# Attention scores of two heads on the two halves of TensorE's rows, and the bias added on VectorE

## The chip, the cores and the metric

The kernel runs on one core of a Trainium2 chip. The metric is the device time of one execution in microseconds (us); the median of the runs counts. A core has a matrix engine (TensorE, PE in the profile, with its weight loads listed apart as PEld), three engines that work element by element (VectorE = DVE, ScalarE = ACT, GpSimd = POOL), and the engine SP, which issues most DMA transfers here. Each engine carries out its own instructions in order; semaphores make one wait for another.

## What is computed

Three layers follow each other, all in float32 at the reference's side. The first is the one that is changed: attention with 4 batches, 8 heads, 576 positions, 64 numbers per head, a window of 128 positions and a bias that falls with distance.

```python
scores = scale * np.matmul(q, k.transpose(0, 1, 3, 2))
bias = slopes[:, None, None] * (-np.abs(rel).astype(np.float32))[None, :, :]
mask = (rel >= 0) & (rel < window)
scores = np.where(mask, scores + bias[None], -1000000000.0)
scores = scores - np.max(scores, axis=-1, keepdims=True)
attn = np.exp(scores)
attn = attn / (np.sum(attn, axis=-1, keepdims=True) + 1e-09)
return np.matmul(attn, v).astype(np.float32)
```

Its output (2304 tokens of 512 numbers) goes through a mixture of 8 experts, `out += P[:, e] * (relu(x @ w1[e]) @ w2[e])`, with weights P from an iterated normalisation over all tokens, and then through one more pair of matrices with a squared relu.

## The kernel before

**Stages.** The attention is worked pair by pair: 4 batches times 4 pairs of heads, in the order of `pairs`. While it runs, the first expert's products for the batches that are done are interleaved; after the last pair come the normalisation of P and the other experts. A run of one expert over one batch is 336 products, each one matmul of 288 columns in float16 with its own weight load (`products`, `hidden`, `layer`). They read `x`, `h` and `w`, write a PSUM bank `ps`, and ScalarE and VectorE add the banks up into `q` (`to_quarter`) and split the sums into two float16 halves for the next product.

**One pair of heads.** It has four units `u` of 128 queries. For each unit `score_ops` writes both heads' scores, 256 columns each, into one PSUM bank: first a matmul of the bias (bfloat16, `bia`) with the identity `identb`, then the scores on top. In the first two batches (`WHOLE = 2`) the scores are float32: `q` of both heads is stored with the other head's 64 rows set to zero, so each matmul uses all 128 rows of the array for one head. A float32 matmul shows as two records in the trace. In the last two batches `make_heads` first splits q and k into float16 halves on ScalarE and VectorE (or GpSimd), and each score is two float16 matmuls, with `qk`/`q` and `kl`.

**The softmax** (`unit`): VectorE takes the negated row maximum of both heads (`nm<-ps`, TENSOR_REDUCE), scales it, ScalarE computes the exponential out of PSUM into `e` and sums it into `sm` on the way (an ACTIVATE and an ACTIVATION_READ_ACCUMULATOR), VectorE adds a small number and inverts the sum, VectorE or ScalarE multiplies. In unit 0 this is done in two segments of 64 and 192 columns, in the others in one of 192. TensorE then transposes `e` into a bank, which is copied to `eT`, and when the pair's four units are there, two groups of 12 matmuls in all (`ps<-eT,v`) give the output (`values`, `take_x`).

**What sets the order.** A greedy scheduler (`Sched`) in the program issues, while the kernel is built, the operation with the lowest key of start time, lead and age, by costs that are written into the code (`START`, `RATE`, `PRICE`). Where an operation may go to two engines, it chooses by these costs. So every engine's order is fixed at build time.

**PSUM** has eight banks, shared out by `FRONT` until the first product run, then `MIDDLE` until the attention's end: P, Q, R for products, S for scores, T for transposes and part of the values, X for the rest of the values. In `MIDDLE` P, Q, R and X have one bank each, S and T two. Other rings: `e` five units (`RE`), `xq` one (`RX`).

## Time and profile before

| | us |
|---|---|
| runs: lowest, median, highest of 3 | 1879.82, 1884.69, 1884.86 |
| profiled execution, time | 1878.17 |
| profiled execution, span from first to last instruction | 1876.4 |
| TensorE busy | 1814.9 (97% of the span) |
| VectorE busy | 1576.8 (84%) |
| ScalarE busy | 1244.3 (66%) |
| GpSimd busy | 169.3 (9%) |

The time of the profiled execution is 1.8 us over its span and 6.5 us under the median. Busy time of TensorE counts an instruction from its start to its modelled end; matmuls are pipelined, so TensorE can be busy without being at its peak, and the distance from one start to the next says what an instruction costs in a dense stretch. The attention with the first products fills the first 285 us. The granted clock is 1.0 (2.4 GHz) there throughout.

### The profile page before, as it was taken

How to read it: one execution, taken by the hardware profiler on the slowest of the kernel's cores; microseconds unless marked ns; L12 is line 12 of the kernel's file. 1: busy time of each engine (PE TensorE's matmuls, PEld its weight loads, DVE VectorE, ACT ScalarE, POOL GpSimd, SP SyncE). 2: the span in 40 equal slices, each digit the busy share in tenths (PEclk: the TensorE clock that was granted, in tenths of full speed). 3: DMA queues.
4: the chain of work that ended last, by engine and by line, in shares of the span. 5: the costliest groups of instructions: out<-in, count | busy, mean ns of one | idle time of the engine just before them, and what ended most of it. 6: DMA issues, size and time to landing. Idle time of an engine off the chain costs nothing.

```text
span 1876.4 us, 38768 instructions
## 1 busy us (share of the span) xinstructions
PE 1814.9 (97%) x15077; PEld 1445.2 (77%) x15077; DVE 1576.8 (84%) x3475; ACT 1244.3 (66%) x3217; POOL 169.3 (9%) x207
## 2 busy tenths in 40 slices
PE   8899999898999999999999999999999999999999
PEld 7778777686777777777777777777777777777777
DVE  7987778897799999999999999999867777666666
ACT  7998876665566666666666667666646566666555
POOL 1110001100101212110012111111000000000000
PEclk9999999998999999999999999999999999999999
DMA  6554412438655535444453555345445585121321
GB/s 164 168 141 109 138 52 74 134 117 253 178 149 151 155 101 159 141 120 118 149 162 93 149 163 164 94 133 147 112 161 146 156 273 178 70 110 63 128 102 70
DMA packets 88233, 255.44 MB, mean 136 GB/s; under 512 B 26992, under 2 KB 35312, under 8 KB 88048
## 3 DMA queue, kind: packets, MB, share of 16 engines
q1 hardware_dynamic: 79984, 219.93, 35.2%
q0 software_dynamic: 8064, 33.03, 9.9%
q8 instruction: 118, 1.93, 0.4%
q14 instruction: 67, 0.55, 0.1%
HBM read 168.57 MB, written 84.35 MB: 135 GB/s over the span
## 4 chain that ended last, share of the span: by engine, by line
PE 60%; DVE 20%; DMA 8%; ACT 7%; issue 4%; SPq 0%; POOL 0%; DVEq 0%; ACTq 0%; POOLq 0%
PE ps L482 60%; DVE h L431 5%; DVE q L431 4%; DVE t L431 3%; ACT q L414 2%; DVE w L446 2%; DMA acc_s<-q 2%; DMA wst<-in_w 2%; DMA x_s<-wo 2%; ACT h L414 1%; ACT e L414 1%; DVE wz L431 1%; DVE wo L446 1%; ACT w L414 1%; DMA yw<-y_s 1%
## 5 line engine op out<-in xcount | busy, mean ns | idle before, releaser
L482 PEld LDWEIGHTS <-w 128*128 128x128 f16 x13440 | 1315.7, 98 | 395.9 <-issue 65.0
L482 PE MATMUL ps<-x,w 128*128 128x288 f16 x6720 | 861.2, 286 | 32.9 <-ACT q L414 19.1
L482 PE MATMUL ps<-h,w 128*128 128x288 f16 x6720 | 857.4, 286 | 14.4 <-DVE q L431 5.8
L414 ACT ACTIVATE q<-ps 128x288 f32<-128x288 f32 x926 | 364.5, 403 | 279.6 <-PE ps L482 268.6
L431 DVE TENSOR_TENSOR q<-ps,q 128x288 f32<-128x288 f32 x672 | 291.5, 449 | 106.5 <-PE ps L482 85.4
L414 ACT ACTIVATE q<-q 128x288 f32<-128x288 f32 x411 | 174.9, 440 | 95.2 <-DVE q L431 93.3
L414 ACT ACTIVATE h<-t 128x576 f16<-128x576 f32 x320 | 212.6, 679 | 30.8 <-DVE t L431 28.3
L414 ACT ACTIVATE h<-q 128x288 f16<-128x288 f32 x480 | 203.8, 439 | 4.4
L414 ACT ACTIVATE w<-wst 128x384 f16<-128x384 f32 (+1 forms) x256 | 141.1, 572 | 80.0 <-DMA wst<-in_w 38.0
L431 DVE TENSOR_TENSOR h<-q,h 128x288 f16<-128x288 f32 x384 | 173.3, 465 | 24.2 <-ACT h L414 23.3
L431 DVE TENSOR_TENSOR h<-t,h 128x576 f16<-128x576 f32 x256 | 188.5, 754 | 1.8 <-ACT h L414 0.9
L446 DVE SCALAR_TENSOR_TENSOR w<-wst,w 128x384 f16<-128x384 f32 (+1 forms) x256 | 161.4, 638 | 8.7 <-ACT w L414 8.4
L431 POOL TENSOR_TENSOR wst<-wst 128x256 f32<-128x256 f32 x107 | 97.1, 909 | 585.4 <-DVE wst L431 334.0
L431 DVE TENSOR_TENSOR t<-q,t 128x288 f32<-128x288 f32 x315 | 140.5, 456 | 1.9 <-ACT q L414 1.0
L431 DVE TENSOR_TENSOR t<-q 128x576 f32<-128x576 f32 x160 | 122.8, 770 | 6.2 <-ACT q L414 4.0
L431 DVE TENSOR_TENSOR q<-q,pb 128x576 f32<-128x576 f32 x108 | 83.6, 784 | 6.3 <-ACT q L414 5.6
L510 POOL DMA_DIRECT2D acc_s<-q x54 | 47.5, 907 | 431.2 <-DVE q L431 404.8
L414 ACT ACTIVATE e<-ps,nm 128x192 f32<-128x192 f32 (+1 forms) x160 | 64.1, 410 | 15.7 <-DVE nm L440 12.7
L431 DVE TENSOR_TENSOR wst<-wst 128x256 f32<-128x256 f32 x149 | 61.8, 426 | 2.4 <-POOL wst L431 0.5
L414 ACT ACTIVATE wo<-wz 128x384 f16<-128x384 f32 x64 | 36.8, 574 | 38.4 <-DVE wz L431 17.7
L453 DVE TENSOR_REDUCE nm<-ps 128x2 f32<-128x384 f32 (+1 forms) x80 | 38.3, 495 | 18.7 <-PE ps L482 18.4
L446 DVE SCALAR_TENSOR_TENSOR h<-q,h 128x288 f16<-128x288 f32 x96 | 43.1, 450 | 12.6 <-ACT h L414 12.6
(94 smaller groups left out, 1059.3 us busy)
## 6 DMA issues: line engine op xcount, KB each, us to landing
x<-x_s SPq DMA_DIRECT2D x56, 1008.0 KB, 4.8
wst<-in_w SPq DMA_DIRECT2D x64, 512.0 KB, 4.7
acc_s<-q POOLq DMA_DIRECT2D x54, 576.0 KB, 6.8
pb<-p_s SPq DMA_DIRECT2D x32, 288.0 KB, 5.5
yw<-in_win SPq DMA_DIRECT2D x16, 512.0 KB, 5.4
yw<-in_wout SPq DMA_DIRECT2D x16, 512.0 KB, 4.9
x_s<-x SPq DMA_DIRECT2D x8, 1008.0 KB, 4.9
win_s<-wo SPq DMA_DIRECT2D x16, 448.0 KB, 3.1
```

Of the source, the lines that this page charges most:

```text
L414: return Op("A", cost, reads, writes, lambda: nc.scalar.activation(out=out, in_=in_, func=func, scale=scale, **k))
L431: lambda: engine(e).tensor_tensor(out=out, in0=in0, in1=in1, op=op),
L446: lambda: nc.vector.scalar_tensor_tensor(out=out, in0=in0, scalar=s, in1=in1, op0=op0, op1=op1),
L453: lambda: nc.vector.tensor_reduce(out=out, in_=in_, axis=axis, op=op, **k),
L482: nc.tensor.matmul(o, l, r, start=start, stop=stop, skip_group_check=True)
L510: return Op("G", 1.04, [in_, out], [out], lambda: nc.gpsimd.dma_start(out=out, in_=in_, accum_op=ALU.add), m, ADDED)
```

## The change

- q and k of a pair are each loaded by one DMA into a tile of 128 rows: rows 0 to 63 are the first head, 64 to 127 the second. Nothing is padded or split; `make_heads` is gone, and so are `WHOLE`, the tiles `q0`, `q1`, `kl` and four memsets on GpSimd.
- A score matmul contracts 64 rows in float32, for all batches. The two heads alternate, head 0 on the array's rows 0 to 63, head 1 on rows 64 to 127, and write different banks. The bias matmuls are gone.
- Two units are worked together (`two`): two S banks, one per head, hold two units each. For each head and segment one VectorE instruction adds the bias to the scores out of PSUM, scales by -1/8, writes the result to `e` in SBUF and keeps its minimum for `nm` (`add_min`); the built program has a second VectorE instruction behind each that writes the minimum out. The scaling of `nm` is gone. ScalarE's exponential reads and writes `e` in SBUF.
- The small operations on `sm` take two units at once. `e` has three tiles of two units, `xq` two, `qk` six, `bia` three.
- PSUM: X is gone, both value groups take T. P has two banks in `MIDDLE` (0 and 7); S and T have four each in `FRONT` and two each in `MIDDLE`.

```diff
-FRONT = dict(zip("PQRSTX", (((0,), 1), ((1,), 1), ((2,), 1), ((0, 1, 3, 4), 4), ((2, 5, 6), 3), ((7,), 1))))
-MIDDLE = dict(zip("PQRSTX", (((0,), 1), ((1,), 1), ((2,), 1), ((3, 4), 2), ((5, 6), 2), ((7,), 1))))
+FRONT = dict(zip("PQRST", (((0,), 1), ((1,), 1), ((2,), 1), ((2, 5, 6, 7), 4), ((0, 1, 3, 4), 4))))
+MIDDLE = dict(zip("PQRST", (((0, 7), 2), ((1,), 1), ((2,), 1), ((5, 6), 2), ((3, 4), 2))))
...
-RE, RX = 5, 1
+RE, RX = 3, 2
...
+    def add_min(out, least, in0, in1, scale):
+
+        return Op(
+            "D", START["D"] + 0.06 + RATE["D"] * size(out), [in0, in1], [out, least],
+            lambda: nc.vector.tensor_tensor_reduce(
+                out=out, in0=in0, in1=in1, scale=scale, scalar=3.0e38, op0=ALU.add, op1=ALU.min, accum_out=least
+            ),
+        )
...
-                        for a in range(2):
-                            yield dma(Q[64 * a : 64 * a + 64, a], qT[b, 2 * p + a])
...
+                    for src in (qT, kT):
+                        x = yield Need(r_qk)
+                        yield dma(x, src[b, h].rearrange("h d s -> (h d) s"))
...
+            def score_ops(at, us, ps):
+
+                Q, K = qk[at]
+                seq = []
+                for j, u in enumerate(us):
+                    q, k = 128 * u + 64, 128 * u - 64
+                    if u == 0:
+                        parts = [(0, 128, 0, 64, 0, 0), (0, 128, 64, 192, q, 0)]
+                    else:
+                        parts = [(0, 64, 0, 64, q, k), (64, 64, 0, 64, q + 64, k + 192), (0, 128, 64, 128, q, k + 64)]
+                    for p0, n, c0, w_, q0, k0 in parts:
+                        for a in range(2):
+                            r = slice(64 * a, 64 * a + 64)
+                            c = 256 * j + c0
+                            seq.append((ps[a][p0 : p0 + n, c : c + w_], Q[r, q0 : q0 + n], K[r, k0 : k0 + w_], True, True))
+                return mms(seq, together=2)
...
-                for i, (c0, c1) in enumerate(segs):
-                    yield reduce(nm[:, 2 * i : 2 * i + 2], ps.rearrange("p (a c) -> p a c", a=2)[:, :, 64 * c0 : 64 * c1], AX.X, ALU.max, True)
-                yield ts(nm[:, :m], nm[:, :m], ISQ, ALU.mult)
...
-                for i, x in each:
-                    yield act(e[x], f[x], AF.Exp, ISQ, nm[:, i : i + 1], sm[:, i : i + 1])
...
+                for i in range(m + 1):
+                    if i < m:
+                        n, a, j, s = each[i]
+                        at_bias = slice(2, 3) if us[j] == 0 and s.start == 0 else s
+                        f = ps[a][:, 256 * j : 256 * j + 256].rearrange("p (c k) -> p c k", k=64)
+                        yield add_min(e[:, j, s, a], nm[:, n : n + 1], f[:, s], t[:, at_bias, a], -ISQ)
+                    if i:
+                        n, a, j, s = each[i - 1]
+                        yield act(e[:, j, s, a], e[:, j, s, a], AF.Exp, -1.0, nm[:, n : n + 1], sm[:, n : n + 1])
...
-                    for r_, part in zip((bank["X"], bank["T"]), parts):
-                        x = yield Need(r_)
+                    for part in parts:
+                        x = yield Need(bank["T"])
```

How the change moves instructions, at three places. First TensorE at the program's start, where `ps_165` and `ps_166` are the banks of units 0 and 1 before, and `ps_160` and `ps_161` those of heads 0 and 1 after. Before:

```order
L482 LDWEIGHTS identb_70
L482 MATMUL ps_165<-bia_163,identb_70 128x2x192
L482 MATMUL ps_165<-qk32_161,q0_144 128x64 x2
L482 MATMUL ps_165<-qk32_161,q0_144 128x192 x2
L482 LDWEIGHTS identb_70
L482 MATMUL ps_166<-bia_163,identb_70 128x2x192
L482 MATMUL ps_166<-qk32_161,q0_144 64x64 x4
L482 MATMUL ps_166<-qk32_161,q0_144 128x128 x2
```

After, the same place:

```order
L491 MATMUL ps_160<-qk_155,qk_151 128x64
L491 MATMUL ps_161<-qk_155,qk_151 128x64
L491 MATMUL ps_160<-qk_155,qk_151 128x192
L491 MATMUL ps_161<-qk_155,qk_151 128x192
L491 MATMUL ps_160<-qk_155,qk_151 64x64
L491 MATMUL ps_161<-qk_155,qk_151 64x64
```

The bias matmuls are gone, and the heads alternate between two banks. Second VectorE in the middle of the attention, among the first expert's products. Before:

```order
L453 TENSOR_REDUCE nm<-ps 128x2 x2
L440 TENSOR_SCALAR nm<-nm 128x2
L431 TENSOR_TENSOR t<-q,t 128x288
L431 TENSOR_TENSOR q_144<-qk_2161,q_144 64x1152
L440 TENSOR_SCALAR nm<-nm 128x4
L431 TENSOR_TENSOR h_2283<-q,h_2283 128x288
L431 TENSOR_TENSOR kl<-qk_2178,q_144 128x1152
```

After, at a similar place (ISA is `add_min`, and behind each the instruction that writes its minimum):

```order
L452 ISA e,nm<-ps,bia 128x3x64
L452 ISA nm 128x1
L465 RECIPROCAL sm<-sm 128x4
L430 TENSOR_TENSOR q<-ps,q 128x288
L430 TENSOR_TENSOR h_551<-q,h_551 128x288
L452 ISA e,nm<-ps,bia 128x3x64
L452 ISA nm 128x1
```

One reduction for two heads has become an add and a write-out per head, and the two splits of 1152 numbers (`q_144`, `kl`) are gone. Third SP's queue of DMA issues at the start. Before:

```order
L506 DMA wgf<-in_wg 128x4x8
L506 DMA q_144<-in_qT 64x576 x2
L506 DMA qk_161<-in_kT 128x576
L506 DMA bia<-in_bias 128x512
L506 DMA q_145<-in_qT 64x576 x2
```

After:

```order
L515 DMA wgf<-in_wg 128x4x8
L515 DMA qk<-in_qT 128x576
L515 DMA qk<-in_kT 128x576
L515 DMA bia<-in_bias 128x512
L515 DMA qk<-in_qT 128x576
```

The first pair's loads take one issue less, and three pairs are loaded ahead of `v` where two were.

## Rows read from the trace of the kernel before

**Rows 1.** By stretch: length, busy PE, PEld, DVE, ACT, POOL (instructions), clock, DMA share, GB/s.
```profile
0.00:58.00 58.00, 48.50 (x422) 41.67 (x423) 44.73 (x148) 46.87 (x170) 11.56 (x22) 1.00 0.64 172
58.00:112.00 54.00, 49.44 (x471) 41.20 (x470) 50.46 (x130) 49.17 (x155) 10.41 (x11) 1.00 0.51 135
112.00:250.00 138.00, 132.79 (x1368) 109.75 (x1365) 108.69 (x281) 120.00 (x376) 2.86 (x3) 1.00 0.46 130
...
600.00:700.00 100.00, 98.80 (x802) 78.18 (x801) 94.48 (x193) 61.73 (x153) 16.28 (x21) 1.00 0.47 131
```
**Rows 2.** Chain that ended last, by time: start, duration, engine and line; 58 to 250.
```profile
75.83 0.67 DVE h L431
...
97.85 1.33 ACT e L414 x7
...
121.77 5.62 PE ps L482 x51
```
**Rows 3.** What TensorE waited for, 58 to 285: us in total, times, longest.
```profile
PE ps L482 <- ACT q L414: 7.5, 12, 1.2
```
**Rows 4.** Instructions in order of time at the start: start, duration, engine.
```profile
3.14 0.43 SPq L506 DMA_DIRECT2D bia<-in_bias  x1
...
6.58 0.58 PE L482 MATMUL ps<-bia,identb 128*128 128x128 bf16 x2 [6.58 <-DMA bia<-in_bias]
...
10.39 0.31 ACT L414 ACTIVATE e<-ps,nm 128x64 f32<-128x64 f32 x1 [7.50 <-DVE nm L440]
```
**Rows 5.** TensorE in order of time, a float32 unit at 16.7 us.
```profile
16.73 0.33 PE L482 MATMUL ps<-bia,identb 128*128 128x384 bf16 x1
16.98 1.10 PE L482 MATMUL ps<-qk,q 128*64 128x64 f32 x12
17.92 0.49 PE L480 MATMUL ps<-ident,e 128*128 128x128 f32 x3
```
**Rows 6.** TensorE in order of time, a float16 unit at 230.1 us.
```profile
230.13 0.33 PE L482 MATMUL ps<-bia,identb 128*128 128x384 bf16 x1
...
230.51 0.21 PE L482 MATMUL ps<-kl,q 128*64 128x64 f16 x2
230.65 0.23 PE L482 MATMUL ps<-q 128*128 128x128 f16 x1
230.71 0.22 PE L482 MATMUL ps<-kl,q 128*128 128x128 f16 x1
...
230.88 0.33 PE L482 MATMUL ps<-bia,identb 128*128 128x384 bf16 x1
```
**Rows 7.** VectorE groups to 290 us: count, busy us, mean ns, idle time before them.
```profile
L453 DVE TENSOR_REDUCE nm<-ps 128x2 f32<-128x384 f32 x64 | 35.0, 547 | 7.7 <-PE ps L482 7.5
...
L453 DVE TENSOR_REDUCE nm<-ps 128x2 f32<-128x128 f32 x16 | 4.6, 286 | 11.0 <-PE ps L482 10.8
...
L440 DVE TENSOR_SCALAR nm<-nm 128x4 f32<-128x4 f32 (+1 forms) x64 | 11.3, 177 | 0.7
...
L440 DVE TENSOR_SCALAR sm<-sm 128x4 f32<-128x4 f32 (+1 forms) x64 | 10.7, 167 | 6.3 <-ACT e L414 6.0
L457 DVE RECIPROCAL sm<-sm 128x4 f32<-128x4 f32 (+1 forms) x64 | 10.4, 163 | 0.8
```
**Rows 8.** ScalarE groups to 290 us, same columns.
```profile
L414 ACT ACTIVATE e<-ps,nm 128x192 f32<-128x192 f32 (+1 forms) x160 | 64.1, 410 | 15.7 <-DVE nm L440 12.7 <-PE ps L482 2.4 <-DVE sm L440 0.4
L414 ACT ACTIVATE e<-e,sm 128x192 f32<-128x192 f32 (+1 forms) x122 | 48.8, 438 | 3.4 <-DVE sm L457 2.1 <-DVE sm L440 1.1
L414 ACT ACTIVATION_READ_ACCUMULATOR e<-ps,nm 128x1 f32 x160 | 34.8, 217 | 0.0
```
**Rows 9.** Instructions on `qk` alone by stretch: each engine's busy time (instructions).
```profile
0.00:58.00 58.00, 26.65 (x239) 21.65 (x240) 0.00 (x0) 0.00 (x0) 1.00 0.64 172
58.00:112.00 54.00, 11.67 (x116) 9.13 (x114) 2.70 (x2) 2.33 (x2) 1.00 0.51 135
112.00:250.00 138.00, 0.00 (x0) 0.00 (x0) 18.95 (x14) 16.26 (x14) 1.00 0.46 130
```

More of the change, by code (lines that the diff above doesn't have):

```diff
@@ L895, in unit @@
                 e = yield Need(r_e)
                 sm = yield Need(r_sm)
[L897 to L900 removed]
+                t = bias_in[at].rearrange("p (a c k) -> p c a k", a=2, k=64)
+                segs = [(j, s) for j, u in enumerate(us) for s in (((0, 1), (1, 4)) if u == 0 else ((0, 3),))]
@@ new lines, in two @@
+                each = [(2 * i + a, a, j, slice(*s)) for i, (j, s) in enumerate(segs) for a in range(2)]
+                m = len(each)
+                for i in range(m + 1):
[7 more added lines that the diff above has]
+                        yield act(e[:, j, s, a], e[:, j, s, a], AF.Exp, -1.0, nm[:, n : n + 1], sm[:, n : n + 1])
@@ L1067, in attn_moe_relu2 @@
             spawn(load_heads(), LEAD_ATT)
-            spawn(make_heads(), LEAD_ATT)
             spawn(units(), LEAD_ATT)
```

137 lines of the change are left out of this document (46 added, 91 removed).

## The prediction

> **What bounds the kernel now.** I read three views in this order. First the busy times by stretch [rows 1], where I call 0 to 58 us stretch A (batch 0 and part of batch 1, no products yet), 58 to 112 stretch B (the rest of batch 1, first products) and 112 to 250 stretch C (batches 2 and 3 in float16, products all along). See who is nearest to the whole length. In A it is ScalarE: its first exponential starts at 10.39 us [rows 4], and of the 47.6 us from there it is busy for some 45. In B VectorE (50.5 of 54) and ScalarE (49.2) are both nearly full, TensorE is at 49.4. In C TensorE is busy for 132.8 of 138, VectorE for 108.7, ScalarE for 120.0.
>
> Second the chain that ended last [rows 2]: up to about 112 us it alternates between short pieces of VectorE and ScalarE, and from 121 us on TensorE's pieces of several microseconds make it up. So time saved on TensorE is worth its full length in C, only as much as the other two engines allow in B, and nothing in A. Third TensorE's waits [rows 3]: from 58 to 285 us its products waited 7.5 us for ScalarE to empty a bank.
>
> After the attention little can move by the order itself: from product 2232 of 13440 on, TensorE's order is the same in both programs, and so are VectorE's last 2485 instructions. The attention's end has 900 products ahead of it before and 984 after. I therefore take the change in time from the first part alone and let it shift the rest.
>
> **The change part by part.** One float32 unit now: the bias matmul starts at 16.73, the scores at 16.98, the next work at 17.92 [rows 5]. That is 1.19 us a unit, 0.94 of it for scores. A pair has four units (unit 0 has other shapes, I take it as alike): 4.76 us, of which 3.76 are scores. A float16 unit goes from 230.13 to 230.88 [rows 6], 0.75, so 3.0 a pair. After the change every pair has 22 float32 matmuls of 64 rows, alternating between the halves. No row shows two matmuls on different halves, so the price lies between 3.76 (no overlap) and 1.88 (full). I take 1.88, since neighbours in the new order never share rows of the array or a bank. Then a float32 pair saves 2.88 and a float16 pair 1.12.
>
> Where the pairs lie follows from the float32 score records [rows 9]: 239 in A and 116 in B, at 44 a pair 5.4 pairs and 2.6. So TensorE is relieved of 15.6 us in A, 7.5 in B and 8 x 1.12 = 9.0 in C.
>
> *A change of shape costs.* In a float16 unit the step from the last 64-column matmuls to the first of 128 columns is 0.14 us from row to row, while 128-column ones follow each other in 0.06 [rows 6]: about 0.08 more. Before, a pair has six such changes; afterwards nine (four in units 0 and 1, five in 2 and 3). Three more, times 10.6 pairs in B and C, times 0.08, is 2.5 us lost.
>
> *VectorE.* Gone are the maxima (35.0 + 4.6), the scaling of `nm` (11.3) and half of the work on `sm` ((10.7 + 10.4) / 2), in all 61.5 us [rows 7]; and the splits, 21.65 us [rows 9]. Added are 128 adds of 192 columns and 32 of 64. The two reductions give (547 - 286) / 256 = 1.02 ns per column and so 0.35 and 0.22 us, 51.8 us. To it come 160 write-outs of the minimum: nothing at the least (hidden in the next instruction's start), at the most what ScalarE's write-out takes, 0.217 [rows 8]; I take 0.163, that of VectorE's own small operations [rows 7], 26.1 us. For adds as long as ScalarE's exponentials (0.410) with that write-out the sum is 160 x 0.627 = 100.3. So a pair costs VectorE (77.9 - 61.5) / 16 = 1.0 us more, with bounds of -0.6 and +2.4.
>
> *ScalarE.* The exponential reads SBUF instead of PSUM; the nearest pair of rows is 438 against 410 ns [rows 8], +0.28 us a pair. The splits go, 18.59 us, of which 2.33 in B and 16.26 in C [rows 9].
>
> *What this makes of A.* TensorE's 15.6 us are cover there, not path. Added are 5.4 x (1.03 + 0.28) = 7.1 us on the two engines that are nearly full. Half of it is 3.5 us of time; VectorE idles for 13.3 us in A [rows 1], but most of that lies before the first scores are done, a little over 9 us; the 4 us left, and some 2 on ScalarE, could take most of the 7.1 and leave 0.5. I take 2 us lost.
>
> *B.* TensorE's 7.5 us can only be used by products, and these need VectorE. From 600 to 700 us, 802 matmuls go with 94.48 us of VectorE [rows 1], 0.118 each. In B VectorE has 3.5 us left; the adds (2.6 x 1.03) and the split that goes (2.70) cancel. That is 30 products, and at 98.80 / 802 = 0.123 us each of TensorE they give 3.6 us later. The new order plans more (330 products, not 252, ahead of batch 1's last values); what VectorE can't follow only lengthens B.
>
> *C.* 9.0 us, all on the path: VectorE and ScalarE lose 18.95 and 16.26 us there and gain 8.2 and 2.2, so neither becomes the bound.
>
> *Start.* TensorE waited until 6.58 for the bias, whose issue ended at 3.57 [rows 4], 3.0 us before. Now it needs q and k alone, each in one issue, so two issues of about half a microsecond less stand ahead; by the same 3.0 us it starts near 5.5. The first exponential, 3.8 us behind, needed two bias matmuls, eight records, two reductions and a scaling, now one matmul pair and one add. I take 2 us, of 1 to 3. The first expert's weights have 14 issues ahead of them on SP, where there were 13, so they don't move; `v` is behind one more pair's loads, about 1.5 us later, and is not read before the first transposes are copied. GpSimd's four memsets hide under these loads.
>
> *Banks.* P has a second bank while products and attention mix. Of the 7.5 us [rows 3] I take 3, of 0 to 7.5. Against it stands that `two` holds both S banks, so no second set of scores can start, and that the values share T; a `two` with half a pair's scores (0.94) and five adds with write-outs (5 x 0.5) holds them for some 3.5 us plus waits, twice a pair, and eight pairs have 138 us, so products cover it.
>
> *The sum:* 9.0 + 3.6 + 2 + 3 - 2.5 - 2 = 13.1 us. The profiled execution took 1878.17, so it would take 1865.1. It lies 6.5 us under the median of the runs shown, 1884.69, and these spread over 5 us; on the median I forecast **1872**.
>
> The Trainium skill, "TensorE: Matmul & The Clock Gate", Part 3, says that matmuls in different row groups run at the same time, but reports 3.07 times for four row tiles, not four. No run here shows that. If two halves gave the same share, 1.53, a pair would cost 2.46, C would give 4.3 instead of 9.0, and the time would be an estimate of 1876.
>
> **The rivals.** *The halves take turns (slower).* If float32 matmuls on the two halves don't overlap, a pair costs 3.76: C gets 8 x 0.76 = 6.1 us longer, B gains 2.6, and with the other terms (+2.5, +2, -5) it is 3.0 us slower, 1888. If each of the 22 moves between halves then also costs 0.08 like a change of shape, a pair costs 5.5: C +20.2, B +2.0, in all +21.7, 1906. It decides from a pair price of 3.5 us on (no gain), and from 4.0 it is slower by 0.3%. For it: no row shows an overlap. Against it: rows and banks are separate. The Trainium skill, "TensorEngine Tiling (Array Packing)", Key Properties, says that changing the mode drains the engine, but not changing the tile within it. The gap at the change of shape agrees; by that rule the moves between halves cost nothing, and this rival ends at 1888, not at 1906.
>
> *The adds cost VectorE what they save (no change).* At 100.3 us they are 38.8 over what goes, 2.4 a pair. In A that is 13.1 us against some 4 of idle time, +9; B gives nothing back; C still gives 9.0 and start and banks 5, the shape changes take 2.5: 2.4 faster, 1882. For it: VectorE and ScalarE alternate on the chain in A and B, and all product sums queue behind the adds on VectorE. Against it: the reductions' own rows give an add 0.35 us, not 0.41.
>
> *All of TensorE's time is used (faster).* 15.6 + 7.5 + 9.0 + 2 + 3 - 2.5 = 34.6, 1850. For it: VectorE and ScalarE choose between themselves who normalises and copies. Against it: they are full in A.
>
> **How the numbers follow.** A measurement can tell about 0.3%, 5.7 us, from no change. Forecast 0.60, by its bounds from 1859 to 1879, so all but faster (0.58, and 0.02 within). All of TensorE's time 0.12, faster. Adds 0.15, within 0.3%. Taking turns 0.13, slower 0.09 and within 0.04. That is faster 0.70, same 0.21, slower 0.09. For 8 in 10 the range takes in the forecast, the adds and half of the most favourable case, 1852 to 1886, and leaves out the halves' turns.
>
> **What would show it.** In the new profile the two records of head 0 and head 1 start closer together than the 0.94 / 12 = 0.08 us of now, and a unit of scores takes under 0.6 us, if they overlap; 0.9 would speak for turns. A VectorE add of 192 columns of 0.35 us and a write-out that moves the next start by at most 0.16 bear out the price; 0.4 each would give the second rival. The attention's last transposes end about 13 us earlier for the products done by then, C's length shrinks most, A's hardly. The prediction is wrong if the granted clock falls in A, where TensorE now has gaps, or if what follows the attention waits for its loads and gives back what came before.

## The result and the profile after

The changed kernel takes 1894.46 us (1890.06 to 1895.96), 1.0063 times the kernel before, 95% interval 1.0049 to 1.0078: slower by some 12 us. The five runs of before beside it have a median of 1880.33, 4 us under the 1884.69 that the prediction started from. The prediction said 1872, range 1852 to 1886. Its profiled execution has a span of 1893.6 us against 1876.4.

By stretch, columns as in [rows 1]:

```profile
0.00:58.00 58.00, 44.38 (x339) 36.32 (x340) 38.93 (x167) 42.92 (x152) 8.81 (x17) 0.91 0.59 170
58.00:112.00 54.00, 49.14 (x445) 39.41 (x444) 46.73 (x139) 48.28 (x146) 8.80 (x10) 0.87 0.32 106
112.00:250.00 138.00, 136.03 (x1356) 111.64 (x1356) 92.53 (x339) 112.43 (x367) 0.00 (x0) 1.00 0.31 98
350.00:400.00 50.00, 40.99 (x313) 31.38 (x312) 48.42 (x129) 32.69 (x77) 1.46 (x2) 0.93 0.39 129
450.00:500.00 50.00, 38.61 (x264) 28.25 (x264) 30.56 (x57) 17.27 (x42) 1.95 (x3) 0.80 0.83 261
```

The same two last stretches in the kernel before:

```profile
350.00:400.00 50.00, 45.70 (x367) 35.56 (x366) 48.70 (x128) 36.38 (x89) 5.83 (x5) 1.00 0.35 119
450.00:500.00 50.00, 46.57 (x356) 35.70 (x355) 35.49 (x70) 23.83 (x61) 3.45 (x4) 0.95 0.88 254
```

The first three rows answer [rows 1]. VectorE and ScalarE are busy for less in all three, in A partly because less of the work is done by 58 us (the table below); TensorE is at least as full in C as before. The last two lie after the attention and hold the loss: TensorE is busy for 41.0 and 38.6 of 50 us, against 45.7 and 46.6.

VectorE's new instructions, from the groups (columns as in [rows 7]):

```profile
L452 DVE CUSTOM_DVE_ANT_0 e<-ps,bia 128x192 f32<-128x192 f32 x128 | 42.4, 351 | 5.5 <-PE ps L491 5.1 <-PE ps L489 0.4
L452 DVE DVE_READ_ACCUMULATOR2_ANT nm<- 128x1 f32 x160 | 13.4, 84 | 0.0
```

And the start, from the timeline (start, length, engine, line, operation, idle time before):

```profile
5.40 5.19 PE L491 MATMUL ps<-qk 64*128 64x64 f32 x46 [5.40 <-DMA qk<-in_kT]
8.28 0.35 ACT L413 ACTIVATE e<-e,nm 128x64 f32<-128x64 f32 x1 [5.29 <-DVE nm L452]
```

The first scores start at 5.40 and the first exponential at 8.28, against 6.58 and 10.39 [rows 4].

**Where the time goes.** I follow TensorE's lost time: the start of product n less n times 0.1229 us, its pace in after where nothing waits (814 products start between 1600 and 1700 us). It counts the attention's own matmuls and all waits. The end of the attention is the start of its last `ps<-eT,v` matmul.

| lost time, us | before | after |
|---|---|---|
| at the end of batch 0 | 54.8 | 58.5 |
| batch 1 | 47.6 | 49.5 |
| batches 2 and 3 | 65.5 | 58.2 |
| at the attention's end | 167.9 | 166.2 |
| from there to product 1500 | 9.3 | 4.6 |
| products 1500 to 1560 | 2.1 | 12.1 |
| products 2130 to 2250 | 11.2 | 18.9 |
| at product 2490 | 193.0 | 204.2 |

So the attention gained 1.7 us instead of 13.1, and two waits behind it lost 18 more than before. At product 2490 the kernel is 11.2 us late, about the difference of the runs; another 5 us go between products 10400 and 11200 in this one execution.

Not all of the two losses is standing still. Behind each wait the granted clock is 0.5 (1.2 GHz) for a while, 6.8 us from 367.3 and 17.1 us from 449.2, and there 18 and 44 products start up to twice as far apart; that is 2.0 of the 12.1 and 5.0 of the 18.9 us (before: 0.2 and 2.9). The rows of after, columns as in [rows 1]:

```profile
350.00:375.00 25.00, 15.99 (x107) 11.31 (x106) 24.96 (x63) 16.95 (x39) 0.00 (x0) 0.86 0.44 146
450.00:475.00 25.00, 15.84 (x94) 10.86 (x94) 16.70 (x33) 10.85 (x26) 0.00 (x0) 0.67 0.75 216
```

The attention ends with 984 products ahead of it where it had 900, and in clock time it ends later, at 287 against 278.5 us. What hangs on it, from the timelines of before and then of after:

```profile
275.54 3.19 PE L482 MATMUL ps<-eT,v 128*128 128x64 f32 x24
287.34 0.30 DVE L453 TENSOR_REDUCE m<-P 128x1 f32<-128x144 f32 x1
289.01 0.27 PE L480 MATMUL ps<-ident,m 128*1 128x128 f32 x1
293.45 0.41 ACT L414 ACTIVATE P<-P,m 128x144 f32<-128x144 f32 x1 [1.12 <-DVE m L440]
```

```profile
286.08 1.32 PE L491 MATMUL ps<-eT,v 128*128 128x64 f32 x10
297.06 1.90 PE L491 MATMUL ps<-wgs,x 128*128 128x16 f16 x60
300.72 0.29 DVE L461 TENSOR_REDUCE m<-P 128x1 f32<-128x144 f32 x1
311.41 0.27 PE L489 MATMUL ps<-ident,m 128*1 128x128 f32 x1
321.88 0.41 ACT L413 ACTIVATE P<-P,m 128x144 f32<-128x144 f32 x1
```

The maximum of P (`m<-P`) comes 13 us later, its transposition 22 us later, since 102 products stand between the last logits and it, where 24 did; the exponential that opens the gate's eight rounds comes 28 us later. Then TensorE's waits in after from 350 to 400 us, and from 440 to 500 us (what waited, for what: us, times, longest):

```profile
PE ps L491 <- DVE cs L461: 4.1, 1, 4.1
PE ps L491 <- DVE q L430: 3.9, 2, 3.6
```

```profile
PE ps L491 <- ACT q L413: 11.0, 2, 10.2
PE ps L491 <- DVE q L430: 1.2, 1, 1.2
PE ps L491 <- ACT h L413: 1.2, 1, 1.2
PE ps L491 <- DVE h L430: 1.0, 1, 1.0
```

The 4.1 us of the first list are a wait for the gate itself: its column sum `cs` on VectorE is late, and the matmul that sums it over the rows stands in TensorE's order among the products (start, length, idle time before):

```profile
368.76 0.60 PE L491 MATMUL ps<-cs,ones 128*128 128x8 f32 x2 [4.15 <-DVE cs L461]
```

The 3.6 us are a wait for VectorE's sum of an earlier product. No wait named here is for weights, and VectorE is busy for 73.4 of the 75 us from 300 on. The wait of 10.2 us is for a buffer `q`: ScalarE, which TensorE waits for, itself waits there for the transfer `acc_s<-q`, which by the code goes out only when that result has been weighted with the gate's result and the early result of its batch has been stored.

### The profile page after: what moved, and what is told of

It is laid out like the page before. It is cut to its first block, busy times and chain, and to the rows that moved or that the text cites. A ratio compares the mean times of both kernels' runs of the same rounds, so it can differ in the third digit from the quotient of the medians.

```text
span 1893.6 us, 38623 instructions
## 1 busy us (share of the span) xinstructions
PE 1820.4 (96%) x14997; PEld 1446.5 (76%) x14997; DVE 1550.4 (82%) x3579; ACT 1236.5 (65%) x3201; POOL 158.2 (8%) x195
## 4 chain that ended last, share of the span: by engine, by line
PE 68%; DVE 17%; DMA 7%; ACT 6%; issue 2%; SPq 0%; POOL 0%; DVEq 0%; ACTq 0%; POOLq 0%
PE ps L491 67%; DVE h L430 5%; DVE t L430 3%; DVE q L430 3%; ACT q L413 2%; DMA acc_s<-q 2%; ACT h L413 2%; DVE w L445 2%; DMA x_s<-wo 2%; DMA yw<-in_win 1%; PE ps L489 1%; ACT e L413 1%; DVE wo L445 1%; DVE wz L430 1%; DMA yw<-y_s 1%
## 5 line engine op out<-in xcount | busy, mean ns | idle before, releaser
L430 DVE TENSOR_TENSOR h<-q,h 128x288 f16<-128x288 f32 x384 | 171.9, 462 | 24.5 <-ACT h L413 23.8
L445 DVE SCALAR_TENSOR_TENSOR w<-wst,w 128x512 f16<-128x512 f32 (+1 forms) x256 | 160.8, 637 | 3.2 <-ACT w L413 2.9
L519 POOL DMA_DIRECT2D acc_s<-q x54 | 47.6, 906 | 444.8 <-DVE q L430 367.2
L413 ACT ACTIVATE e<-e,nm 128x192 f32<-128x192 f32 (+1 forms) x160 | 67.8, 425 | 10.9 <-DVE nm L452 10.6
L452 DVE CUSTOM_DVE_ANT_0 e<-ps,bia 128x192 f32<-128x192 f32 (+1 forms) x160 | 47.8, 325 | 22.8 <-PE ps L491 22.2
L491 PE MATMUL ps<-qk 64*64 64x64 f32 (+3 forms) x704 | 56.0, 311 | 8.0 <-DMA qk<-in_kT 5.4
L413 ACT ACTIVATE wo<-wz 128x384 f16<-128x384 f32 x64 | 36.8, 574 | 39.3 <-DVE wz L430 17.5
```

Of the source, the lines that this page charges most:

```text
L413: return Op("A", cost, reads, writes, lambda: nc.scalar.activation(out=out, in_=in_, func=func, scale=scale, **k))
L430: lambda: engine(e).tensor_tensor(out=out, in0=in0, in1=in1, op=op),
L445: lambda: nc.vector.scalar_tensor_tensor(out=out, in0=in0, scalar=s, in1=in1, op0=op0, op1=op1),
L452: lambda: nc.vector.tensor_tensor_reduce(out=out, in0=in0, in1=in1, scale=scale, scalar=3.0e38, op0=ALU.add, op1=ALU.min, accum_out=least),
L491: nc.tensor.matmul(o, l, r, start=start, stop=stop, skip_group_check=True)
L519: return Op("G", 1.04, [in_, out], [out], lambda: nc.gpsimd.dma_start(out=out, in_=in_, accum_op=ALU.add), m, ADDED)
```

## The experiments

**How two halves and shapes are priced.** Two kernels hold the same score matmuls as the changed one, in another order inside a set; all else stays.

```diff
+                wide = lambda x: x[1].shape[-1] == 128
+                seq.sort(key=lambda x: wide(x) if us[0] else not wide(x))
                 return mms(seq, together=2)
```

> The changed kernel with the same matmuls in another order within each set of scores: those of one shape stand together (in units 0 and 1 the 128-column stationary tiles first, in units 2 and 3 the 64-column ones first), still alternating between the heads, so that a pair has 4 changes of shape inside its scores instead of 9. Everything else stands where it stood. If a change of shape costs about 0.23 us (the gaps that TensorE's weight loads show there), a pair's scores take some 1.7 to 2.2 us instead of 2.84, and the time falls by 4 to 8 us if TensorE's time in the attention is what counts, 1886 to 1890, or by less than 2 us if the later wait for the gate sets the end. If a change costs 0.08 as the prediction had it, the pair takes 2.4 or more and the time stays within 2 us of the changed kernel.

```diff
-                return mms(seq, together=2)
+                return mms(seq[0::2] + seq[1::2], together=2)
```

> The changed kernel without the alternation: all score matmuls of head 0 of a set, then all of head 1; the same matmuls, the same banks, the same place in the program. If neighbours on different halves overlap in the changed kernel, that overlap is gone: a pair's scores go from 2.84 us to between 3.8 and 4.7, and the time rises by 10 to 20 us, 1904 or more. If the halves take turns anyway, a pair's scores and the time stay as they are, within 3 us.

TensorE's weight loads in the timeline, of after, of the grouped kernel and of the one with a head at a time:

```profile
128.63 0.52 PEld L491 LDWEIGHTS ps<-qk 64*128 64x128 f32 x8 [0.24 <-issue]
129.38 0.58 PEld L491 LDWEIGHTS ps<-qk 64*64 64x64 f32 x12 [0.23 <-issue]
130.07 0.31 PEld L489 LDWEIGHTS ps<-ident,e 128*128 128x128 f32 x3
136.12 1.27 PEld L491 LDWEIGHTS ps<-qk 64*64 64x64 f32 x24 [0.24 <-issue]
137.52 0.31 PEld L489 LDWEIGHTS ps<-ident,e 128*128 128x128 f32 x3
```

```profile
123.47 1.18 PEld L491 LDWEIGHTS ps<-qk 64*128 64x128 f32 x20 [0.24 <-issue]
124.71 0.31 PEld L489 LDWEIGHTS ps<-ident,e 128*128 128x128 f32 x3
130.76 0.92 PEld L491 LDWEIGHTS ps<-qk 64*64 64x64 f32 x24 [0.24 <-issue]
131.80 0.31 PEld L489 LDWEIGHTS ps<-ident,e 128*128 128x128 f32 x3
```

```profile
135.67 2.59 PEld L491 LDWEIGHTS ps<-qk 64*64 64x64 f32 x24 [0.17 <-issue]
138.38 1.92 PEld L491 LDWEIGHTS <-w 128*128 128x128 f16 x12
146.07 0.52 PEld L491 LDWEIGHTS ps<-qk 64*128 64x128 f32 x4 [0.24 <-issue]
146.81 0.79 PEld L491 LDWEIGHTS ps<-qk 64*64 64x64 f32 x10 [0.23 <-issue]
147.82 0.56 PEld L491 LDWEIGHTS ps<-qk 64*64 64x64 f32 x6 [0.23 <-issue]
148.50 0.31 PEld L489 LDWEIGHTS ps<-ident,e 128*128 128x128 f32 x3
```

From the first load to the next work, units 0 and 1 take 1.45 us in after, units 2 and 3 take 1.04 grouped, units 0 and 1 take 2.43 a head at a time. With the other half of the pair (1.39, 1.25, 2.71) a pair is 2.84, 2.29 and 5.14 us. A pair has 9, 6 and 15 changes of tile shape, entering and leaving a set counted. If every change costs the same, the first two give 0.183 us a change and 1.19 us of matmuls; the third then leaves 5.14 - 15 x 0.183 = 2.39, twice 1.19. The single records agree: in after two weight loads of 64*128 start 0.007 us apart every 0.10 us, a head at a time one starts every 0.11; and at a change the next load stands 0.16 to 0.21 us later than it would in a row of one shape, also where the merged rows above show no gap. So two heads on two halves overlap in full, and each change of shape costs some 0.18 us. The Trainium skill, "TensorEngine Tiling (Array Packing)", Key Properties, says that a change of the mode drains the engine and a change of the tile in it doesn't; the gaps of 0.23 us in these rows, and the 0.007 us between the halves, agree.

The grouped kernel takes 1887.31 us, 1.0026 (1.0009 to 1.0042), 7 us under the changed one; a head at a time takes 1929.89, 1.0261 (1.0232 to 1.0289), 35 above it and more than expected, since that order also adds six changes of shape. For 16 pairs 0.55 and 2.30 us each would be 8.8 and 36.8: a pair's scores count with almost their whole length, in A and B too.

**P's second bank.**

```diff
-MIDDLE = dict(zip("PQRST", (((0, 7), 2), ((1,), 1), ((2,), 1), ((5, 6), 2), ((3, 4), 2))))
+MIDDLE = dict(zip("PQRST", (((0,), 1), ((1,), 1), ((2,), 1), ((5, 6), 2), ((3, 4), 2))))
```

> The changed kernel, but P keeps one bank while products and attention mix (bank 7 stays empty); everything else of the change stays. The planner then puts 972 products ahead of the attention's end instead of 984, and 1164 ahead of P's maximum become about 1160 less what the one bank holds back; ahead of the first transposes of the early results' weights 1896 instead of 1968. Theory 'gate late': the gate's last steps come several us earlier and the time falls by 6 to 12 us against the changed kernel, 1882 to 1888. Rival 'attention dearer': nothing of the scores, the adds or the first 112 us is changed, the time stays within 4 us of the changed kernel, 1890 to 1898.

It takes 1883.10 us, 1.0003 (0.9990 to 1.0015). Built, it has 840 products ahead of the attention's end, not 972, the number that stands ahead of P's maximum: I had mixed the two up. By its own lost time its attention is dearer than after's, 172.1 against 166.2, but it ends at 275.4 us, and what follows is cheap: 1.2 us at products 1500 to 1560, 10.4 at 2130 to 2250. The stretches from 250, 350 and 450 us:

```profile
250.00:285.00 35.00, 34.22 (x292) 28.78 (x291) 28.17 (x68) 27.20 (x73) 0.00 (x0) 1.00 0.19 67
350.00:400.00 50.00, 48.43 (x392) 37.97 (x390) 49.02 (x131) 35.77 (x89) 4.04 (x5) 1.00 0.34 118
450.00:500.00 50.00, 46.23 (x357) 35.82 (x356) 34.67 (x68) 24.09 (x61) 3.45 (x4) 0.96 0.84 257
```

With 11 us given back by one number, the loss hangs on P's second bank: on the 144 products that it puts ahead of the attention's end, or on which bank it is (tried below). One row of after shows what they do there; VectorE idles while TensorE works off products:

```profile
285.61 0.46 DVE L430 TENSOR_TENSOR q<-ps,q 128x288 f32<-128x288 f32 x1 [9.46 <-PE ps L491]
```

**Both edits**, the sort and the one bank, together.

> Both edits at once: scores grouped by shape and P with one bank while products and attention mix. P's maximum stands behind 972 products, the gate's result behind 1896. If a pair's scores cost 1.19 us plus 0.18 for each change of shape (what the three score orders run so far give: 6, 9 and 15 changes at 2.29, 2.84 and 5.14 us), 3 changes less on 10 pairs give 5 to 6 us, and if the gate's place and the scores add up, the time is 5 to 7 us under that of the one-bank kernel: 1876 to 1879, faster than the kernel before by 0.2 to 0.35%. If what follows the attention gives the gain back here too, it stays at 1882 to 1885.

Grouped scores with one P bank take **1874.01 us, 0.9958 (0.9943 to 0.9973)**: faster than both kernels. The edits add up: 9 us against one bank alone, 13 against grouping alone.

**What counts is when the attention ends.** Over these kernels and the next ones:

| kernel | products ahead | attention's end, us | 128th piece of weights ready | product 2490 | median |
|---|---|---|---|---|---|
| before | 900 | 278.5 | +86.4 | +220.5 | 1882.6 |
| after | 984 | 287.1 | +82.9 | +223.1 | 1894.5 |
| one P bank | 840 | 275.4 | +86.2 | +223.0 | 1883.1 |
| grouped | 984 | 277.5 | +82.9 | +223.3 | 1887.3 |
| both | 840 | 268.9 | +86.0 | +222.3 | 1874.0 |
| a head at a time | 984 | 328.0 | +82.9 | +224.0 | 1929.9 |
| gate's lead | 984 | 290.5 | +86.4 | +223.9 | 1897.6 |

(The median of before is that of the runs beside these kernels. Columns with + count from the attention's end; a piece is a record of `w<-wst` on ScalarE or VectorE, and 128 of them make the first two experts.) In these kernels product 2490 starts 220 to 224 us after the attention's end, whether 840 or 984 products are done by then, though 144 products are 17.7 us of TensorE's time. So products done ahead of that end earned nothing here. For product 2490 this doesn't hold in all the later kernels with 858 to 984 products ahead: it comes as early as 207 us after the end with two banks swapped. But the median lies 1600 to 1610 us behind the attention's end of the trace in 16 of the 17 kernels of this document with 840 to 984 products ahead; in the other, the changed kernel without the gate's rounds, it is 1597. This is a regularity of medians and single traces (with after's order of the attention its end lies between 287.0 and 291.9 us in six of them), not a mechanism. In the code two things start at that end: the gate, which needs the last batch, and the second expert's weights, for which six places (`SPARE`) are added in the memory that the attention leaves. The 65th piece comes 7.3 us after the end in after, 7.8 in before.

**Is it the gate?** First in the kernel before, a wait added:

```diff
-            yield lambda: state["logits"] == B
+            yield lambda: state["logits"] == B and state["products"] >= 1080
```

> The kernel before, with one wait added and nothing else: the gate's column and row steps after its logits may not start until 1080 products have been issued (in the kernel before P's maximum stands behind 960 products, in the changed kernel behind 1164; with the added wait it stands behind 1104). No score, bias or bank is touched. Theory 'gate late' (the changed kernel is slower because its gate's steps start some 13 us later, and the products of the next stretch later run dry waiting for what the gate weights): the time rises by about 8 to 12 us, 1888 to 1893, and between 440 and 500 us TensorE is busy less, with a lower granted clock, than in the kernel before. Rival 'attention dearer' (float32 scores on half the rows and the clock in the first 112 us lost the time): the steps' start has slack, the time stays within 3 us of before, 1878 to 1884.

1884.32 us, 1.0019 (1.0008 to 1.0030). The gate's exponential came 26 us later (319.3) and its result 11 us, about as in after, but only 2 us were lost: the planner knew of the wait and put its result behind 1992 products. Then the changed kernel with the gate's steps earlier, alone and grouped:

```diff
-LEAD_ATT, LEAD_LOGIT, LEAD_W0, LEAD_GATE, LEAD_WEIGH = -0.2988, -0.1623, -0.5925, -0.2787, 0.2666
+LEAD_ATT, LEAD_LOGIT, LEAD_W0, LEAD_GATE, LEAD_WEIGH = -0.2988, -0.1623, -0.5925, -0.15, 0.2666
```

> The changed kernel with one number of the planner other, the gate's lead, -0.15 instead of -0.2787: the gate's steps win more ties, so that the transposes of its result stand behind 1698 products instead of 1968; the attention keeps its order and its price, P's maximum stands behind 1158 products instead of 1164. Theory 'gate late' (the products run dry behind the gate's result and the loads of what it weights, so TensorE time saved in the attention is given back there): the first weighting of an early result comes 10 us or more before that of the changed kernel, TensorE's wait of 10 us after 446 us shrinks, and the time falls by 6 to 12 us, 1882 to 1888. Rival 'attention dearer' (the score matmuls and the clock alone set the loss): within 3 us of the changed kernel, 1891 to 1898. Rival 'VectorE full' (from 300 to 400 us VectorE is busy without a gap, and gate steps that come earlier only push the product sums back): no gain or slower, 1892 to 1902.

> Scores grouped by shape and the gate's lead at -0.15 (its result behind 1698 products instead of 1968), P with two banks as in the changed kernel. The attention of the grouped kernel ended some 11 us of TensorE's time earlier than in the kernel before. Theory 'gate late': these 11 us are kept for the most part: 1871 to 1879. Rival 'VectorE full': the gain is given back, 1884 to 1890, as with the grouped scores alone.

1897.58 us (1.0078, 1.0056 to 1.0100) and 1888.03 (1.0031, 1.0018 to 1.0043): nothing won. The first weighting came 23 us earlier and the second wait shrank from 18.9 to 11.1 us, but the first grew from 12.1 to 17.4, and TensorE lost another 6 between products 1560 and 2130. The theory that the gate alone sets the end fell here.

A third bank for T in place of P's second, with grouped scores:

```diff
+MIDDLE = dict(zip("PQRST", (((0,), 1), ((1,), 1), ((2,), 1), ((5, 6), 2), ((3, 4, 7), 3))))
```

> Scores grouped by shape, P with one bank and the freed bank 7 given to the transposes and values (T gets three banks): attention's end behind 858 products, P's maximum behind 954, the gate's result behind 1818. Theory 'gate late': as the grouped kernel with one P bank or better by 0 to 4 us, 1872 to 1879. Rival 'VectorE full': 1881 to 1886.

1881.95 us, 0.9996 (0.9984 to 1.0007), 8 above the version with bank 7 left empty. Its attention ends at 273.4 us with 858 products ahead, and product 2490 comes 214.2 us later, 3.6 us before that version's; then 8.4 us are lost up to product 3000, and to what is not known.

**Fewer products ahead.** If they earn nothing, the attention should go first, here in the changed kernel and with grouped scores.

```diff
-LEAD_ATT, LEAD_LOGIT, LEAD_W0, LEAD_GATE, LEAD_WEIGH = -0.2988, -0.1623, -0.5925, -0.2787, 0.2666
+LEAD_ATT, LEAD_LOGIT, LEAD_W0, LEAD_GATE, LEAD_WEIGH = 0.0, -0.1623, -0.5925, -0.2787, 0.2666
```

> The changed kernel with one number of the planner other, the attention's lead, 0.0 instead of -0.2988: fewer products are put ahead of the attention, 660 instead of 984 ahead of its last values; the gate's result stays behind 1956 products (1968). Theory 'attention's end' (in every kernel run so far the median is the attention's end in the trace, 269 to 328 us, plus 1602 to 1610 us, with 840, 858, 900 or 984 products ahead of it alike: products done ahead of the end are worth nothing later): the end moves from 287 to some 247 us and the time falls to between 1853 and 1875, less than the whole 40 us since with so few products done TensorE's own time must set the end at some point. Rival 'gate late': the gate's result stands where it stood, the products run dry behind it as before, 1885 to 1895. Rival 'attention dearer': the attention's matmuls cost what they cost wherever they stand, 1890 to 1897.

> The same lead of 0.0 with the scores grouped by shape. Theory 'attention's end': faster than with the lead alone by 0 to 9 us (3 changes of shape fewer on each of 16 pairs, 0.18 us each), 1848 to 1872, and faster than the kernel before by more than 0.5%. If products done ahead do count (the other theories), it stays at 1880 to 1888, as with the grouped scores alone.

1898.40 us (1.0085, 1.0053 to 1.0116) and 1892.55 (1.0051, 1.0032 to 1.0070). The attention ends at 257.0 and 253.5 with 660 products ahead, but product 2490 comes 261 and 259 us later. TensorE's lost time at that end is 175.9 us, since it idles where products used to fill gaps, and the last logits come at 289.6 us, behind 852 products. For the median the rule holds between 840 and 984 products, not at 660.

**Without the gate's rounds.** Seven of eight rounds left out, before and after:

```diff
-            for it in range(8):
+            for it in range(1):
```

> The kernel before with one of the gate's eight rounds of column and row sums instead of eight: seven rounds are left out, each some 2.3 us of VectorE between 294 and 407 us and one hop over TensorE. It is the control for the next run; by itself the time may fall by 5 to 25 us, since VectorE is nearly full between 300 and 400 us.

> The changed kernel with the same seven rounds left out, to be compared with the kernel before without them. If the wait for the gate's rounds, or VectorE's load from them, is what made the products done early worthless, the two lie within 4 us of each other (the attention of the changed kernel ends 8.6 us later with 84 products more, 10.3 us, done). If neither is, the changed kernel stays 9 to 14 us the slower, as with all eight rounds.

1888.66 us (1.0033, 1.0016 to 1.0049) and 1883.60 (1.0000, 0.9983 to 1.0017). The sign turns: the changed kernel is now 5 us ahead. But the control became 6 us slower with less work, as its gate's result moved from behind 1896 to behind 1122 products and all that follows with it, so the pair doesn't say which of the gate's waits or VectorE's load it was. It is the one pair in which the early products count: product 2490 comes 209.6 us after the attention's end in the changed kernel and 221.1 in its control, 11.5 us apart for 84 products worth 10.3. That points at the gate's rounds, or at VectorE's work on them, as part of what made early products worthless; the changed order of the control keeps it from being shown.

**Is it VectorE's load?** It is busy for 48.4 of 50 us from 350 us on. Two kernels leave work of VectorE out without moving an instruction, first the sums over raw weights (the same in before), then, for the second expert alone, also the subtraction of the halves:

```diff
+            if part:
+                x[1].issue = lambda a=a: nc.vector.tensor_tensor(out=a[0][:, 0, 0:16], in0=a[1][:, 0, 0:16], in1=a[2][:, 0, 0:16], op=a[3])
...
+        if part:
+            op.issue = lambda: nc.vector.tensor_copy(lo, hi)
```

> The changed kernel with VectorE's sums over the second and third experts' raw weights (in place, 256 columns, 0.415 us each, 44 of them between 285 and 450 us) cut to 16 columns; the rest of these sums is left out. Nothing moves: every instruction stands where it stood on its engine. At about 0.1 us each that takes some 13 us of VectorE's 18.3 us there away. Theory 'VectorE full' (from the attention's end to 440 us VectorE is the bound, and what it has not done by 300 us is the loss): the time falls by 7 to 14 us against the changed kernel, 1880 to 1888, and TensorE's waits of 4.1 and 3.6 us for VectorE between 350 and 375 us shrink or go. Rival 'gate late' alone (the wait for the gate's result and the loads behind it): less than 3 us, 1891 to 1897, unless the gate's rounds, which run on VectorE, come earlier with it; the first weighting of an early result would then show it, 442 us in the changed kernel.

> The control: the kernel before with the same sums cut to 16 columns (42 of them on VectorE between 285 and 450 us, 17.5 us). Theory 'VectorE full': VectorE bounds this stretch here too (44.7 of 50 us busy from 300, 48.7 from 350), the time falls by 4 to 12 us, 1870 to 1879. If VectorE isn't the bound in the kernel before, it stays within 3 us.

> The changed kernel with VectorE's share of the second expert's weights made cheap: its sums over the raw weights cut to 16 columns, and the low halves of the split weights copied from the high halves instead of subtracted; both parts of the computation are left out. Nothing moves in the order, ScalarE and the loads keep their work. In every kernel so far the 128th conversion of weights ended 74 to 86 us after the attention, and product 2490 came 219 to 225 us after it, whether 840 or 984 products were ahead. Theory 'second expert's weights': TensorE, ahead by its early products, waits at products 1500 to 1560 for that work (12 us lost there, 2 in the kernel before); it falls to under 5 us and the time by 5 to 9 us, 1885 to 1889, if the gate's result behind it comes earlier with TensorE's order; if the gate's result doesn't come earlier, its wait at products 2130 to 2250 (19 us lost in the changed kernel) grows by what is gained and the time stays at 1891 to 1896. If the loads or ScalarE set the pace of these weights, the 12 us stay and so does the time.

1893.89 us (1.0058, 1.0042 to 1.0073), 1878.92 (0.9982, 0.9966 to 0.9999) and 1891.71 (1.0064, 1.0047 to 1.0081). Up to product 2490 VectorE is busy for some 10 us less in the first two and 15 in the third; the medians fall by 0.6, 3.3 and 2.8 us. For the two changed kernels that is nothing clear: their ratios to before, 1.0058 and 1.0064, lie on both sides of after's 1.0063. In the last one the 128th piece is ready 78.1 us after the attention's end instead of 82.9, product 1560 comes 5.0 us sooner after that end, and still 8.9 us are lost at products 1500 to 1560 (TensorE's waits from 350 to 400 us):

```profile
PE ps L491 <- DVE cs L461: 3.7, 1, 3.7
PE ps L491 <- DVE q L430: 2.2, 2, 1.7
```

So VectorE's load alone doesn't set it. Handing such sums to GpSimd in the best version didn't help either:

```diff
-'GW': 0.465
+'GW': 0.3
```

> The best version so far (grouped scores, one P bank) with one price of the planner changed: GpSimd is asked to take these sums over raw weights at 0.3 instead of 0.465 us, so that it takes 86 of them more and VectorE fewer; the plan shifts with it (786 products ahead of the attention's end instead of 840, the gate's result behind 1758 instead of 1896). Theory 'VectorE full': VectorE has less left to do after 300 us, the time falls by 2 to 8 us against that version, 1866 to 1872. Rival: GpSimd needs twice VectorE's time for each sum and the weights come later, 1874 to 1882.

1882.01 us, 0.9998 (0.9983 to 1.0014), 8 slower than the best version. With 786 products ahead product 2490 comes 235.5 us after the attention's end, so there the rule no longer holds either.

**Is it bank 7?** The gate's small matmuls use bank 7 after the attention (`BACK`), and there P's products sit in the changed kernel.

```diff
-MIDDLE = dict(zip("PQRST", (((0, 7), 2), ((1,), 1), ((2,), 1), ((5, 6), 2), ((3, 4), 2))))
+MIDDLE = dict(zip("PQRST", (((0, 3), 2), ((1,), 1), ((2,), 1), ((5, 6), 2), ((4, 7), 2))))
```

> The changed kernel with two banks swapped while products and attention mix: P has banks 0 and 3 instead of 0 and 7, T has 4 and 7 instead of 3 and 4. Both keep two. Bank 7 is the one that the gate's small matmuls use once the attention has ended, in both kernels; in the changed kernel products of P sit in it, with the swap it is free as soon as T lets it go. The attention keeps its order to the last row (984 products ahead of its end, 1062 ahead of the last logits); P's maximum stands behind 1110 products instead of 1164 and the gate's result behind 2034 instead of 1968. Theory 'bank 7' (the gate starts late because its bank is P's, and in every kernel with the result behind 1944 to 1998 products, product 2490 is issued 77 to 82 us after the gate's last transpose): the maximum's transpose comes near 305 us instead of 311, the products up to 2490 some 6 to 12 us earlier, and the time is 1881 to 1889. If VectorE's load or the attention's price set the loss, 1890 to 1897.

> The same swap with the scores grouped by shape. Theory 'bank 7': the 7 us that the grouping gave and the swap's gain add up, 1873 to 1882, and it may pass the one-bank version with grouped scores (1874). Otherwise 1884 to 1890, as with the grouped scores alone.

The gate does start earlier, in the timeline of the kernel with the swap:

```profile
302.97 0.29 DVE L461 TENSOR_REDUCE m<-P 128x1 f32<-128x144 f32 x1
307.05 0.27 PE L489 MATMUL ps<-ident,m 128*1 128x128 f32 x1
316.11 0.40 ACT L413 ACTIVATE P<-P,m 128x144 f32<-128x144 f32 x1
```

4.1 us from the maximum to its transposition instead of 10.7, the wait at products 2130 to 2250 falls from 18.9 to 2.7 us, and product 2490 comes 14 us earlier. But 11.7 us are then lost between products 2490 and 3000, where after loses none, and the kernels take 1892.57 us (1.0054, 1.0036 to 1.0072) and 1883.80 (1.0009, 0.9996 to 1.0021): 2 and 3.5 us less than without the swap, with intervals that overlap. That bank 7 held up the gate is shown, that it is the cause of the loss is not: with 984 products ahead and bank 7 free, the time stays.

**What stays open.** The two waits stand in a row, and easing one left or moved the other. That the end of the program follows the attention's end is shown by the medians; by what step is not. By the profile TensorE's first wait is for VectorE, at a product's sum and at the gate's column sum, and VectorE's order mixes these with the conversions of the second expert's weights; what holds that order up (its own load, the loads of the weights, ScalarE's share or SP's queue) was not parted. In after the twelfth load of weights is issued 35.7 us after the end, in before 18.6.

## Why the prediction was wrong, step by step

- **"After the attention little can move by the order itself ... let it shift the rest."** This is the step that failed most. The order from product 2232 on is the same, but the time at which it can run hangs on the attention's end, and that came 8.6 us later. To let a gain shift the rest is to count 84 products more as 10 us won; by the table they were worth nothing, and two waits behind the attention took 31 us where they took 13. And of the 13.1 us only 1.7 were there to be shifted: A, B and C below fell short by 3.7, 4.9 and 2.8. The prediction named this at its end ("if what follows the attention ... gives back what came before") and gave it no chance and no price.
- **Banks.** P's second bank gained what I allowed in the attention, 5.9 us of lost time between one bank and two (I took 3 of 0 to 7.5). Its sign on the whole is the other: it lets 144 products in ahead of the end, and taking it away makes the kernel 11 us faster.
- **The change of shape, 0.08, and three more a pair.** It is 0.18 by three orders of the same matmuls. The 0.08 was read from float16 rows; in the records of the float32 unit of [rows 5] the first load of 128 columns stands 0.21 us behind the last of 64, where those of 64 follow each other within 0.05. And I halved 3.76 us, which holds the six changes of the old shapes, as if a drain overlapped too. Predicted 1.88 + 0.24 = 2.12 us a pair, measured 2.84. So a pair in C saves some 0.16 us against the 3.0 of [rows 6], not 0.88: 1.3 instead of 7.0 us for eight pairs. The overlap of the halves itself, on which rival one turned, was predicted right and is complete, though by the prediction's own sign (a unit under 0.6 us, or 0.9) it would have stayed open: a unit takes 0.71. The Trainium skill's ratio of four row tiles ("TensorE: Matmul & The Clock Gate", Part 3), taken as a share, would have made it 1.53, an estimate; measured is 2.39 / 1.19 = 2.0.
- **"TensorE's 15.6 us are cover there, not path" (A).** Wrong: a head at a time made batch 0 end 8.2 us later, of the 9.2 that its four pairs cost more. (Grouping shows 3.2 us earlier in the table's trace, but this end varies: 58.3 to 61.2 us in six traces of this order, 55.3 to 59.2 in three grouped ones, 54.3 to 56.9 in four of the kernel before's.) With scores, add, exponential and transposes of a `two` in a chain, their price counts in A as in C. A lost 3.7 us where 2 lost and 2 won at the start were forecast.
- **B** was to win 3.6 us, 3.0 less the shapes, and lost 1.9 (measured over batch 1). More products were taken in, as planned (330), but they lengthened it, and with one P bank it lost 7.3. **C** won 7.3 of the 10.1 forecast (9.0 + 3 less 1.9 for shapes): 1.3 are the scores, 2.5 the bank (with one it won 4.8), and the rest, which may be the splits that VectorE and ScalarE no longer do, was not tried apart.
- **VectorE's price**: the add was right, 351 ns against 0.35; the write-out, 84 ns against 0.163, was taken at twice its size. So a pair costs VectorE 0.2 us more instead of 1.0, and the second rival was not what happened. **The start** was right: 2.1 us earlier at the first exponential.
- **The granted clock** fell in A and B (0.91 and 0.87), as the last paragraph feared: it is 0.5 for 10.2 us from 39.6 us on and for 6.8 us each from 67.0 and 104.5; from 33 to 40 us TensorE was busy for 4.9 of 7 us, in the kernel before for all 7. The kernel with both edits shows 0.91 and 0.94 there and is the fastest, so it doesn't decide the sign. What it costs in A and B was not tried apart. As an estimate, half of these 23.8 us is the most, 12 us, more than the 5.6 that A and B lost, so it stays a rival for that part.
- **The chances.** Slower had 0.09, all from the halves taking turns. The mechanism that came, a saving that lets filler work in ahead of a join, was not among the rivals.

The best version's rows for C, 350 and 450 us, for comparison with those at the top:

```profile
112.00:250.00 138.00, 131.69 (x1360) 110.18 (x1358) 91.66 (x353) 112.18 (x372) 0.00 (x0) 1.00 0.31 102
350.00:400.00 50.00, 48.49 (x394) 38.20 (x393) 49.10 (x131) 36.16 (x89) 2.75 (x3) 1.00 0.32 108
450.00:500.00 50.00, 46.99 (x368) 36.54 (x367) 37.02 (x74) 25.91 (x66) 3.46 (x4) 0.97 0.73 216
```

## What to carry to other kernels

Where a stage ends in a join (memory given back, a global step that needs the last batch), look for the time at which that join comes, not for how much other work is done by then; a buffer or a saving that lets filler work in ahead of the join can cost more than it wins, and the built order shows how much stands ahead of the join before any run. Count changes of the array's tile shape as a price of their own when matmuls get smaller, and group them. Where instructions are placed by a planner, taking work away moves the rest, so a control with the same edit belongs to each such experiment, and an edit that keeps the order says more.

## What was not expected of the hardware

Two float32 matmuls on the two halves of the rows overlap in full (2.39 against 1.19 us a pair), while each change of tile shape around them costs 0.18 us, so that in the changed kernel 1.65 of a pair's 2.84 us are changes of shape. The granted clock showed half speed in stretches of A and B in which TensorE had gaps (10.2 us from 40 us on in the records of after), though it was 1.0 there before; what that cost is open.
